# Largest weight over the 128 partitions: by two passes through TensorE, or by a small tensor in memory

## The chip, the cores and the metric

The kernel runs on one core of a Trainium2 chip. The metric is the device time of one execution in microseconds (us). A core has engines that each take their own instructions in order: TensorE (PE, matrix products; PEld is its weight load), VectorE (DVE), ScalarE (ACT), GpSimd (POOL) and SyncE (SP, which here only issues transfers). They wait for each other by semaphores. Transfers between the core's memory and the chip's memory (DRAM) run on 16 DMA engines beside them.

## The reference

A linear recurrence over time (RWKV) gives tokens `x`, and a mixture of 8 experts is applied to every token, weighted by a gate that eight rounds of row and column normalisation (Sinkhorn) balance:

```python
x = attn_out.transpose(0, 2, 1, 3).reshape(3072, 384)      # _attn_ref: recurrence over 768 steps
logits = x @ w_gate                                        # 3072 x 8
P = np.exp(logits - logits.max())
for _ in range(8):
    P /= P.sum(1, keepdims=True) + 1e-09
    P /= P.sum(0, keepdims=True) + 1e-09
    P *= N / E
out = np.zeros((N, D))
for e in range(E):                                         # 8 experts
    h = np.maximum(x @ w1[e], 0.0)                         # 384 x 1024
    out += P[:, e:e + 1] * (h @ w2[e])                     # 1024 x 384
```

## The kernel before

**Numbers.** Products run in 16-bit floats, and each operand is split into a high and a low half (three products for one). So that the halves fit, weights are first scaled by a power of two that follows from the largest absolute weight. The largest value has to be known on all 128 partitions, and this step is the one that changes.

**Stages.** The recurrence comes first and computes expert 0 beside it. Then come 14 stages, one for each half of experts 1 to 7. A stage multiplies tokens and weights in a scheme with 15 products in place of 18 (`g1_slots`: 15 slots of three matmuls each, with VectorE and ScalarE adding up the results from PSUM banks named bA, bY, bZ, bC, bB into `tb`, `hbx`, `hb`), for two groups of tokens `g` and two column halves `j`. That makes 60 slots a stage. Between the slots stand the matmuls of the second product of the group before (`po`), five or four after each slot. Their results are scaled (`stg`) and added to `accd` in DRAM by transfers that POOL issues. The stretch between the end of the recurrence and stage 0 is called the passage below. It works off the rest of expert 0 (`ph`, `po`), runs the Sinkhorn rounds (`rs`, `pc`, `cs`, `pm`) and prepares the first weights and the second group of tokens.

**Order.** Every engine's instructions stand in the order in which the program is written. In a stage, `stage_tasks` hangs the steps for the next stage's weights on slots (`at(19, ...)`). In the passage, a table of `ticks` does the same: a tick runs its steps and then one unit of expert 0, which is nine `ph` or twelve `po` matmuls.

**The next stage's weights** (`stage_weights`), by slot: `load` at 0 (two transfers into `rawb`), `pool` sums into `ucb` on POOL, `amax` at 9, 10, 17, 18 (VectorE, largest of a partition's weights, into `wms`), `reduce_max` at 19 (`wmas`, 128 x 2), `across` at 21, `scale` at 23 (`isw`, `sw`), and from slot 30 on `high` (ScalarE) and `low` (VectorE), which write the two halves into `ws`. `across` and `scale` use `over_partitions`: TensorE transposes `wmas` into two rows of 128 (`pmax_s`), VectorE takes the largest of each row (`mt_s`) and puts the two on a diagonal (`md_s`), and a product with ones brings them to all partitions, from where `scale` reads them. The PSUM bank for this comes from the pool that `small_` names.

**Tokens in the passage** (`plan_tokens`): VectorE puts the halves of tokens together (`rebuild`, `ucb<-hbx`, three times), POOL makes 17 sums from them (`pool`, into `tb`), and ScalarE and VectorE split these in four parts into `xv`. This is done twice in the passage, for token groups 2 and 3, in the same buffers `ucb` and `tb`; the weights of stage 0 use `ucb` in between.

Of the kernel before, what the change touches and what calls it, by code (L numbers as in the profile page):

```python
# [8 lines left out]
F32 = mybir.dt.float32  # L9
# [3 lines left out]
ALU = mybir.AluOpType  # L13
AX = mybir.AxisListType
# [18 lines left out]
def rwkv_sinkhorn_moe(  # L33
# [13 lines left out]
    V, S_, G, T, Q = (  # L47
        InOrder(tc, e) for e in (nc.vector, nc.scalar, nc.gpsimd, nc.tensor, nc.sync)
    )
# [3 lines left out]
    E, _, F = w1.shape  # L53
    P = 128
# [6 lines left out]
    TB = 512  # L61
# [10 lines left out]
    sm = ctx.enter_context(tc.tile_pool(name="sm", bufs=2))  # L72
    stgp = ctx.enter_context(tc.tile_pool(name="stgp", bufs=3))
    dram = ctx.enter_context(tc.tile_pool(name="dram", bufs=1, space=bass.MemoryType.DRAM))
    ps1 = ctx.enter_context(tc.tile_pool(name="ps1", bufs=2, space=PSUM))
    ps2 = ctx.enter_context(tc.tile_pool(name="ps2", bufs=2, space=PSUM))
# [37 lines left out]
        return v_[:, :, t % TH, :]  # L114

    accd = dram.tile([NT, DM], F32, name="accd")
    e0d = [dram.tile([NT, DM], F32, name=f"e0d{j}") for j in range(2)]
    logits = const.tile([P, NTT, E], F32, name="logits")
    inv_s = const.tile([P, NTT], F32, name="inv_s")
# [6 lines left out]
    def pow2_scale(m, inv, s, down):  # L126
        V.tensor_scalar(inv, m, 1e-30, down, op0=ALU.max, op1=ALU.mult)
        V.tensor_single_scalar(
            inv.bitcast(I32), inv.bitcast(I32), EXP_MASK, op=ALU.bitwise_and
        )  # L130
        V.reciprocal(s, inv)


    def over_partitions(m, n, pool, tag, name):

        pt = pool.tile([P, TB], F32, tag=tag, name=f"pmax_{name}")
        T.transpose(pt[:n, :P], m, ident)
        mt = sm.tile([P, 1], F32, tag="mt", name=f"mt_{name}")
        V.tensor_reduce(mt[:n], pt[:n, :P], axis=AX.X, op=ALU.max)
        md = sm.tile([P, 2], F32, tag="md", name=f"md_{name}")  # L140
        V.tensor_scalar_mul(md[:n, :n], ident[:n, :n], mt[:n])
        yield pt[:, 2 * P : 2 * P + n]
        T.matmul(pt[:, 2 * P : 2 * P + n], ones[:n, :], md[:n, :n], start=True, stop=True)
        yield pt[:, 2 * P : 2 * P + n]
# [474 lines left out]
    def add(o, x_, y_):  # L619
        return lambda: G.tensor_tensor(o, x_, y_, op=ALU.add)  # L620

    def sub(o, x_, y_):
        return lambda: G.tensor_tensor(o, x_, y_, op=ALU.subtract)
# [133 lines left out]
    ps4 = ctx.enter_context(tc.tile_pool(name="ps4", bufs=4, space=PSUM))  # L757
# [3 lines left out]
    ucb = big.tile([P, 11 * TS], F32, name="ucb")  # L761
    tb_ = big.tile([P, 13 * TS], F32, name="tb")
# [5 lines left out]
    def stage_weights(s):  # L768
        e, half = 1 + s // 2, s % 2
        home = ws0 if s % 2 == 0 else ws1  # L770
        w1s = part(home, F16, 0, (NPR, 2, TS))
        w2s = part(home, F16, NPR * 2 * TS, (2, FHC, DM))
        isw = sm.tile([P, 2], F32, tag="isw", name=f"isw_{s}", bufs=3)
        sw = sm.tile([P, 2], F32, tag="sw", name=f"sw_{s}")
        m = sm.tile([P, 4], F32, tag="wm", name=f"wms_{s}")
        ma = sm.tile([P, 2], F32, tag="wma", name=f"wmas_{s}")
        uc = part(ucb, F32, 0, (11, TS))

        def load():
            fs = slice(half * FH, (half + 1) * FH)  # L780
            Q.dma_start(raw1, w1[e][:, fs].rearrange("(c p) f -> p c f", p=P))
            Q.dma_start(raw2, w2[e][fs, :].rearrange("(c p) d -> p c d", p=P))

        def amax(i):
            n = KC * FH // 2
            V.tensor_reduce(
                m[:, i : i + 1], rawb[:, i * n : (i + 1) * n],
                axis=AX.X, op=ALU.max, apply_absolute_value=True,
            )

        res = []

        def reduce_max():
            V.tensor_reduce(ma, m.rearrange("p (j i) -> p j i", i=2), axis=AX.X, op=ALU.max)

        def across():
            res.append(over_partitions(ma, 2, *small(), f"s{s}"))
            next(res[0])

        def scale():  # L800
            pow2_scale(next(res[0]), isw, sw, 0.25)

        a = [raw1[:, i % KC, (i // KC) * TS : (i // KC + 1) * TS] for i in range(6)]
        u_ = {r_: uc[:, UI[r_]] for r_ in US[:11]}
        pool = [
            add(u_[0], a[0], a[2]), sub(u_[7], a[3], a[0]), add(u_[1], u_[7], a[4]),
            sub(u_[2], u_[1], a[1]), sub(u_[10], a[2], a[1]), add(u_[3], u_[2], u_[0]),
            sub(u_[8], a[5], u_[10]), add(u_[9], a[3], a[5]), sub(u_[12], a[4], u_[8]),
            sub(u_[13], a[2], a[5]), add(u_[14], a[0], a[5]),
        ]  # L810
        pieces = [
            (w1s[:, i : i + n], uc[:, i : i + n], 0) for i, n in ((0, 3), (3, 3), (6, 3), (9, 2))
        ] + [
            (w1s[:, 11:13], raw1[:, 0:2, :TS], 0), (w1s[:, 13:15], raw1[:, 1:3, TS:], 0)
        ] + [
            (w2s[:, :, i : i + 2].rearrange("p l c d -> p c l d"), raw2[:, i : i + 2], 1) for i in (0, 2)
        ]

        def high(i):
            o, x_, j = pieces[i]  # L820
            S_.activation(o[:, :, 0], x_, AF.Copy, scale=sw[:, j : j + 1])

        def low(i):
            o, x_, j = pieces[i]
            V.scalar_tensor_tensor(
                o[:, :, 1], x_, sw[:, j : j + 1], o[:, :, 0], op0=ALU.mult, op1=ALU.subtract
            )

        return dict(w1s=w1s, w2s=w2s, isw=isw, load=load, amax=amax, reduce_max=reduce_max, across=across,
                    scale=scale, pool=pool, high=high, low=low, n=len(pieces))  # L830


# [38 lines left out]
    def at(t, *fs):  # L871
        ticks.setdefault(t, []).extend(fs)

    small_ = [(ps2, "po")]

    def small():
        return small_[0]

    WS = {0: stage_weights(0)}
    sk = sinkhorn()  # L880
    at(0, WS[0]["load"])
# [7 lines left out]
    def plan_tokens(sg, t_build, t_pool, pool_rate, t_parts, homes):  # L889
        rebuild, singles, pool, high, low = combine_tokens(sg, *homes)  # L890
        for th, t in enumerate(t_build):
            at(t, lambda th=th: rebuild(th))
        at(t_build[-1], singles)
        for i, f in enumerate(pool):
            at(t_pool + i // pool_rate, f)
        for (i, n), t in zip(((0, 3), (3, 3), (6, 3), (9, 4)), t_parts):
            at(t, lambda i=i, n=n: high(i, n))
            at(t + 1, lambda i=i, n=n: low(i, n))

    plan_tokens(2, (0, 1, 2), 3, 3, (5, 7, 8, 10), (ucb, 0, tb_, 0))  # L900
    W0 = WS[0]
    for i, t in enumerate((4, 5, 9, 10)):
        at(t, lambda i=i: W0["amax"](i))
    at(11, W0["reduce_max"])
    at(12, W0["across"])
    for i, f in enumerate(W0["pool"]):
        at(9 + i // 3, f)
    at(14, W0["scale"])
    for n, i in enumerate((0, 1, 2, 3, 4, 5, 6, 7)):
        at(15 + n, lambda i=i: W0["high"](i))  # L910
        at(16 + n, lambda i=i: W0["low"](i))
    plan_tokens(3, (20, 20, 21), 21, 3, (24, 26, 27, 29), (ucb, 0, tb_, 0))

    tick = 0
    while units or any(t >= tick for t in ticks):
# [172 lines left out]
    def stage_tasks(s):  # L1088
        ts = {}

        def at(t, *fs):
            ts.setdefault(t, []).extend(fs)

        def gate():
            pes[s] = gate_of(1 + s // 2, WS[s]["isw"], s)

        at(2, gate)
        if s == 0:
            at(3, gate0)
        if s + 1 < NS:  # L1100
            w_ = WS[s + 1] = stage_weights(s + 1)
            at(0, w_["load"])
            for i, t in enumerate((9, 10, 17, 18)):
                at(t, lambda i=i: w_["amax"](i))
            for i, f in enumerate(w_["pool"]):
                at(8 + i, f)
            at(19, w_["reduce_max"])
            at(21, w_["across"])
            at(23, w_["scale"])
            for i, (th_, tl) in zip(  # L1110
                (4, 6, 0, 7, 1, 5, 2, 3),
                ((0, 2), (1, 3), (8, 9), (8, 10), (15, 17), (16, 18), (23, 24), (23, 25)),
            ):
                at(NSLOT + th_, lambda i=i: w_["high"](i))
                at(NSLOT + tl, lambda i=i: w_["low"](i))
        else:
            for _ in range(2 * FHC):
                at(20, load_final)
        for n in range(4):
            n4 = (s - 2) * 4 + n  # L1120
            if 0 < n4 <= NTT:
                at(15 * n + 2, flush(n4 - 1)[1])
                at(15 * n + 3, flush(n4 - 1)[2])
            if 0 <= n4 < NTT:
                at(15 * n + 8, flush(n4)[0])
        return ts
# [4 lines left out]

    rest = e0_rest()
    late = None
    small_[0] = (ps4, "pq")
    for s in range(NS):
        tasks = stage_tasks(s)
        for g in range(NG):
            for j in range(2):
                for n, nxt in enumerate(g1_slots(s, g, j)):
# [3 lines left out]
                    i = j * NPR + n  # L1143
# [37 lines left out]
```

## Time and profile before

| what | value |
|---|---|
| median of 3 runs | 1607.06 us (1606.31 to 1610.93) |
| the profiled execution | 1606.63 us, of which the span from the first to the last instruction is 1604.9 us |
| TensorE busy | 1575.5 us, 98% of the span |
| VectorE, ScalarE, GpSimd busy | 1019.4, 668.0 and 587.7 us |
| mean granted TensorE clock | 0.991 |

Rows of the profile read like this. In a timeline: start, duration, engine, line, operation, what it writes and reads with the shape, how many alike in a row, and in square brackets the idle time before it with what ended it. In a list of groups: busy time in all, mean ns of one, idle time before them. All work on the compute engines and all transfers of the kernel bear line 29, a helper that records the order, so the names of the tiles tell operations apart. In the list of transfers the last number is the median time from issue to landing, in us.

### The profile page before, as it was taken

How to read it: one execution, taken by the hardware profiler on the slowest of the kernel's cores; microseconds unless marked ns; L12 is line 12 of the kernel's file. 1: busy time of each engine (PE TensorE's matmuls, PEld its weight loads, DVE VectorE, ACT ScalarE, POOL GpSimd, SP SyncE). 2: the span in 40 equal slices, each digit the busy share in tenths (PEclk: the TensorE clock that was granted, in tenths of full speed). 3: DMA queues.
4: the chain of work that ended last, by engine and by line, in shares of the span. 5: the costliest groups of instructions: out<-in, count | busy, mean ns of one | idle time of the engine just before them, and what ended most of it. 6: DMA issues, size and time to landing. Idle time of an engine off the chain costs nothing.

```text
span 1604.9 us, 24284 instructions
## 1 busy us (share of the span) xinstructions
PE 1575.5 (98%) x9423; PEld 912.8 (57%) x9423; DVE 1019.4 (64%) x1706; ACT 668.0 (42%) x1190; POOL 587.7 (37%) x688
## 2 busy tenths in 40 slices
PE   7899999989999999999999999999999999999999
PEld 5777787655455555555555555555555555555555
DVE  6676756674766666666666666666666666656554
ACT  2233333343544445454535454544444453535320
POOL 6566675452020342424242424243242424242200
PEclk8899999999999999999999999999999999999999
DMA  7233330212022556565665656564545454545434
GB/s 181 48 70 76 85 86 26 86 42 89 30 94 55 105 83 115 84 122 84 123 89 85 115 83 120 85 114 58 94 55 94 56 97 54 96 55 89 60 89 132
DMA packets 163899, 136.60 MB, mean 85 GB/s; under 512 B 88257, under 2 KB 158018, under 8 KB 163778
## 3 DMA queue, kind: packets, MB, share of 16 engines
q0 software_dynamic: 44928, 61.36, 30.9%
q1 hardware_dynamic: 118640, 73.63, 15.8%
q8 instruction: 75, 1.23, 0.3%
q14 instruction: 46, 0.38, 0.1%
q10 hardware_dynamic: 210, 0.00, 0.0%
HBM read 53.69 MB, written 80.22 MB: 83 GB/s over the span
## 4 chain that ended last, share of the span: by engine, by line
PE 94%; DVE 3%; ACT 1%; issue 1%; ACTq 0%; DVEq 0%
PE po L29 46%; PE bZ L29 11%; PE bY L29 11%; PE ph L29 5%; PE bB L29 4%; PE bA L29 4%; PE py L29 4%; PE bC L29 2%; PE pA L29 1%; PE pu L29 1%; PE prT L29 1%; PE pz L29 1%; PE pkT L29 1%; DVE ws L29 0%; PE px L29 0%
## 5 line engine op out<-in xcount | busy, mean ns | idle before, releaser
L29 PE MATMUL po<-ws,hbx 128*128 128x384 f16 x3360 | 736.9, 326 | 0.0
L29 POOL DMA_DIRECT2D accd<-stg x288 | 250.4, 870 | 700.7 <-ACT stg L29 682.8
L29 PEld LDWEIGHTS <-hbx 128*128 128x128 f16 x3576 | 337.1, 98 | 287.4
L29 PEld LDWEIGHTS <-ws 128*128 128x128 f16 x3096 | 303.4, 98 | 249.6 <-issue 8.3
L29 ACT ACTIVATE hbx<-tb 128x512 f16<-128x512 f32 x224 | 141.1, 630 | 444.3 <-DVE tb L29 444.3
L29 PE MATMUL po<-ws,hb 128*128 128x384 f16 x1248 | 323.0, 327 | 2.3 <-DVE ws L29 2.3
L29 DVE TENSOR_TENSOR tb<-bY,tb 128x512 f32<-128x512 f32 x168 | 116.2, 692 | 193.9 <-PE bY L29 192.8
L29 ACT ACTIVATE stg<-po,pe 128x384 f32<-128x384 f32 x312 | 179.5, 575 | 127.9 <-PE po L29 101.0
L29 PE MATMUL bZ<-xv,ws 128*128 128x512 f16 x840 | 227.0, 379 | 0.8 <-DVE tb L29 0.7
L29 PE MATMUL bY<-xv,ws 128*128 128x512 f16 x840 | 227.0, 379 | 0.1
L29 DVE TENSOR_TENSOR tb<-bZ,tb 128x512 f32<-128x512 f32 x168 | 115.5, 687 | 133.1 <-PE bZ L29 133.1
L29 PEld LDWEIGHTS <-hb 128*128 128x128 f16 x1248 | 122.4, 98 | 96.1 <-issue 4.9
L29 POOL TENSOR_TENSOR ucb<-rawb 128x256 f32<-128x256 f32 x84 | 75.1, 945 | 94.0 <-DMA rawb<-in_moe_w_dram 94.0
L29 DVE TENSOR_TENSOR tb<-bB,tb 128x512 f32<-128x512 f32 x112 | 77.5, 692 | 49.7 <-PE bB L29 47.8
L29 PE MATMUL ph<-hbx,ws 128*128 128x384 f16 x576 | 106.1, 333 | 1.2 <-DVE hb L29 1.2
L29 DVE SCALAR_TENSOR_TENSOR hbx<-tb,hbx 128x512 f16<-128x512 f32 x112 | 78.6, 702 | 24.2 <-ACT hbx L29 19.5
L29 DVE SCALAR_TENSOR_TENSOR hb<-tb,hbx 128x512 f16<-128x512 f32 x112 | 77.2, 690 | 24.6 <-ACT hbx L29 19.5
L29 PE MATMUL bA<-xv,ws 128*128 128x512 f16 x336 | 90.8, 379 | 1.0 <-ACT tb L29 1.0
L29 PE MATMUL bB<-xv,ws 128*128 128x512 f16 x336 | 90.8, 379 | 0.0
L29 DVE SCALAR_TENSOR_TENSOR hb<-ph,hb 128x384 f16<-128x384 f32 x64 | 35.5, 555 | 60.8 <-ACT hb L29 60.6
L29 ACT COPY tb<-bZ 128x512 f32<-128x512 f32 x56 | 32.8, 586 | 68.2 <-PE bZ L29 68.2
L29 ACT ACTIVATE hb<-ph 128x384 f16<-128x384 f32 x64 | 31.5, 492 | 60.3 <-PE ph L29 59.0
(163 smaller groups left out, 1647.6 us busy)
## 6 DMA issues: line engine op xcount, KB each, us to landing
accd<-stg POOLq DMA_DIRECT2D x288, 192.0 KB, 3.7
rawb<-in_moe_w_dram SPq DMA_DIRECT2D x28, 768.0 KB, 7.4
e0d<-stg SPq DMA_DIRECT2D x48, 192.0 KB, 2.0
hb<-e0d SPq DMA_DIRECT2D x48, 192.0 KB, 3.4
rn<-in_r_dram SPq DMA_DIRECT2D x24, 192.0 KB, 3.1
kn<-in_k_dram SPq DMA_DIRECT2D x24, 192.0 KB, 3.3
vn<-in_v_dram SPq DMA_DIRECT2D x24, 192.0 KB, 2.7
accd<-stg SPq DMA_DIRECT2D x24, 192.0 KB, 1.8
```

Of the source, the lines that this page charges most:

```text
L29: return lambda *a, **k: self.tc.keep_in_program_order(f(*a, **k))
```

## The change

For the 14 stages, `over_partitions` is no longer used (the gate, the maximum of the logits and expert 0's own weights keep it). `reduce_max` now also starts a transfer on SP that writes `wmas` to a DRAM tensor `wmx` of its own for each stage: 256 elements of 4 bytes. `across` is a second transfer on SP, which reads those 256 numbers back into each of the 128 partitions (1 KB each), in a part of `tb` that the stages leave free. It waits for the first to land. `scale` has VectorE take the two maxima from the 256 numbers (`wmj`) and goes on as before. In a stage the steps stand at slots 19, 20 and 25 instead of 19, 21 and 23. In the passage they stand at ticks 10, 11 and 15 instead of 11, 12 and 14; `high` and `low` of stage 0's weights and the second `plan_tokens` stand one tick later.

```diff
+    wmx = dram.tile([2 * E, 2, P], F32, name="wmx")
...
-        res = []
+        mb = tb_[:, 5 * TB : 5 * TB + 2 * P]
 
         def reduce_max():
             V.tensor_reduce(ma, m.rearrange("p (j i) -> p j i", i=2), axis=AX.X, op=ALU.max)
+            Q.dma_start(wmx[s].rearrange("j p -> p j"), ma)
 
         def across():
-            res.append(over_partitions(ma, 2, *small(), f"s{s}"))
-            next(res[0])
+            Q.dma_start(
+                mb, wmx[s].rearrange("(o j) p -> o (j p)", o=1).broadcast_to([P, 2 * P])
+            )
 
         def scale():
-            pow2_scale(next(res[0]), isw, sw, 0.25)
+            mj = sm.tile([P, 2], F32, tag="wmj", name=f"wmj_{s}")
+            V.tensor_reduce(mj, mb.rearrange("p (j q) -> p j q", q=P), axis=AX.X, op=ALU.max)
+            pow2_scale(mj, isw, sw, 0.25)
...
-    at(11, W0["reduce_max"])
-    at(12, W0["across"])
+    at(10, W0["reduce_max"])
+    at(11, W0["across"])
...
-    at(14, W0["scale"])
+    at(15, W0["scale"])
...
-    plan_tokens(3, (20, 20, 21), 21, 3, (24, 26, 27, 29), (ucb, 0, tb_, 0))
+    plan_tokens(3, (21, 21, 22), 22, 3, (25, 27, 28, 30), (ucb, 0, tb_, 0))
...
-            at(21, w_["across"])
-            at(23, w_["scale"])
+            at(20, w_["across"])
+            at(25, w_["scale"])
```

VectorE in the passage, before, from the last `amax` on (`hb<-ph` splits a result of expert 0, `xv<-tb` a part of the tokens, `rs` begins a Sinkhorn round):

```order
L29 TENSOR_REDUCE wms_6990<-rawb 128x1
L29 SCALAR_TENSOR_TENSOR hb_73<-ph_5_7207,hb_73 128x384
L29 TENSOR_TENSOR xv_6983<-tb,xv_6983 128x4x256
L29 TENSOR_REDUCE wmas_6991<-wms_6990 128x2
L29 TENSOR_REDUCE rs_7240<-pm 128x24
```

The same place now:

```order
L29 TENSOR_REDUCE wms_6991<-rawb 128x1
L29 TENSOR_REDUCE wmas_6992<-wms_6991 128x2
L29 SCALAR_TENSOR_TENSOR hb_73<-ph_5_7210,hb_73 128x384
L29 TENSOR_TENSOR xv_6984<-tb,xv_6984 128x4x256
L29 TENSOR_REDUCE rs_7243<-pm 128x24
```

`wmas` has moved ahead of two instructions, and TensorE, which had its transposition of `wmas` between two units of expert 0, has nothing there now.

VectorE later in the passage, before (`ws<-rawb` are `low` steps of stage 0's weights, `ucb<-hbx` the three `rebuild` steps of the second `plan_tokens`, `cs` to `pm` half a Sinkhorn round):

```order
L29 TENSOR_TENSOR ucb<-hbx 128x2x3x128 x2
L29 SCALAR_TENSOR_TENSOR ws_74<-rawb,sw_6989,ws_74 128x2x256
L29 TENSOR_TENSOR ucb<-hbx 128x2x3x128
L29 SCALAR_TENSOR_TENSOR hb_73<-ph_3_7428,hb_73 128x384
L29 TENSOR_REDUCE cs_7442<-pc_7440 128x8
L29 TENSOR_SCALAR cs_7442<-cs_7442 128x8
L29 RECIPROCAL cs_7442<-cs_7442 128x8
L29 TENSOR_TENSOR pm<-pm,cs_7442 128x192
L29 SCALAR_TENSOR_TENSOR ws_74<-rawb,sw_6989,ws_74 128x768
L29 SCALAR_TENSOR_TENSOR hb_73<-ph_4_7452,hb_73 128x384
L29 SCALAR_TENSOR_TENSOR ws_74<-rawb,sw_6989,ws_74 128x768
L29 TENSOR_REDUCE rs_7484<-pm 128x24
```

The same place now:

```order
L29 TENSOR_TENSOR ucb<-hbx 128x2x3x128 x2
L29 SCALAR_TENSOR_TENSOR hb_73<-ph_3_7416,hb_73 128x384
L29 TENSOR_REDUCE cs_7430<-pc_7428 128x8
L29 TENSOR_SCALAR cs_7430<-cs_7430 128x8
L29 RECIPROCAL cs_7430<-cs_7430 128x8
L29 TENSOR_TENSOR pm<-pm,cs_7430 128x192
L29 SCALAR_TENSOR_TENSOR ws_74<-rawb,sw_6990,ws_74 128x2x256
L29 TENSOR_TENSOR ucb<-hbx 128x2x3x128
L29 SCALAR_TENSOR_TENSOR hb_73<-ph_4_7445,hb_73 128x384
L29 SCALAR_TENSOR_TENSOR ws_74<-rawb,sw_6990,ws_74 128x768
L29 TENSOR_REDUCE rs_7478<-pm 128x24
```

The third `rebuild` stands behind an `hb` and a `cs` group that it stood ahead of, and the last `low` has gone behind the `rs` that ends this piece.

VectorE at slots 19 to 25 of a stage, before:

```order
L29 TENSOR_REDUCE wmas_9125<-wms_9124 128x2
L29 TENSOR_TENSOR tb<-bZ_0_1_9336,tb 128x512
L29 SCALAR_TENSOR_TENSOR hbx<-tb,hbx 128x512
L29 TENSOR_TENSOR tb<-bC_0_1_9390,tb 128x512
L29 TENSOR_REDUCE mt_s_9398<-pmax_s_9396 2x1
L29 TENSOR_SCALAR md_s_9400<-ident,mt_s_9398 2x2
L29 TENSOR_TENSOR tb<-bY_0_1_9325,tb 128x512
L29 SCALAR_TENSOR_TENSOR hbx<-tb,hbx 128x512
L29 TENSOR_TENSOR tb<-bZ_0_1_9336,tb 128x512
L29 TENSOR_SCALAR isw_9122<-pmax_s_9396 128x2
L29 TENSOR_SCALAR isw_9122<-isw_9122 128x2
L29 RECIPROCAL sw_9123<-isw_9122 128x2
```

The same place now:

```order
L29 TENSOR_REDUCE wmas_9117<-wms_9116 128x2
L29 TENSOR_TENSOR tb<-bZ_0_1_9328,tb 128x512
L29 SCALAR_TENSOR_TENSOR hbx<-tb,hbx 128x512
L29 TENSOR_TENSOR tb<-bC_0_1_9384,tb 128x512
L29 TENSOR_TENSOR tb<-bY_0_1_9317,tb 128x512
L29 SCALAR_TENSOR_TENSOR hbx<-tb,hbx 128x512
L29 TENSOR_TENSOR tb<-bZ_0_1_9328,tb 128x512
L29 TENSOR_REDUCE wmj_9435<-tb 128x2
L29 TENSOR_SCALAR isw_9114<-wmj_9435 128x2
L29 TENSOR_SCALAR isw_9114<-isw_9114 128x2
L29 RECIPROCAL sw_9115<-isw_9114 128x2
```

`mt_s` and `md_s` are gone and `wmj` is new. Although `scale` is written two slots later, it stands behind the same `tb<-bZ` as before, since VectorE has no other work in those two slots.

SP in the same stage now (`hb<-e0d` fetches a piece of expert 0's result; before, the two middle rows were not there):

```order
L29 DMA hb_73<-e0d_79 128x384
L29 DMA hb_73<-e0d_80 128x384
L29 DMA wmx<-wmas_9117 128x2x1
L29 DMA tb<-wmx 128x256
L29 DMA hb_73<-e0d_79 128x384
```

The fetches behind the new pair now stand behind the wait of `tb<-wmx` for the landing of `wmx`. GpSimd's instructions stand as before.

More of the change, by code (lines that the diff above doesn't have):

```diff
@@ L872, in at @@
         ticks.setdefault(t, []).extend(fs)
-    small_ = [(ps2, "po")]
-    def small():
-        return small_[0]
     WS = {0: stage_weights(0)}
@@ L903, in rwkv_sinkhorn_moe @@
         at(t, lambda i=i: W0["amax"](i))
-    at(11, W0["reduce_max"])
-    at(12, W0["across"])
+    at(10, W0["reduce_max"])
+    at(11, W0["across"])
     for i, f in enumerate(W0["pool"]):
         at(9 + i // 3, f)
-    at(14, W0["scale"])
+    at(15, W0["scale"])
     for n, i in enumerate((0, 1, 2, 3, 4, 5, 6, 7)):
-        at(15 + n, lambda i=i: W0["high"](i))
-        at(16 + n, lambda i=i: W0["low"](i))
-    plan_tokens(3, (20, 20, 21), 21, 3, (24, 26, 27, 29), (ucb, 0, tb_, 0))
+        at(16 + n, lambda i=i: W0["high"](i))
+        at(17 + n, lambda i=i: W0["low"](i))
+    plan_tokens(3, (21, 21, 22), 22, 3, (25, 27, 28, 30), (ucb, 0, tb_, 0))
     tick = 0
@@ L1133, in rwkv_sinkhorn_moe @@
     late = None
-    small_[0] = (ps4, "pq")
     for s in range(NS):
```

## The prediction, made before the change was run

> **What bounds the kernel now.** I read the page's summary and its chain of waits first, then the waits of TensorE, then busy times by stretch, then the timelines around the step that changes.
>
> ```profile
> span 1604.9 us, 24284 instructions
> PE 1575.5 (98%) x9423; PEld 912.8 (57%) x9423; DVE 1019.4 (64%) x1706; ACT 668.0 (42%) x1190; POOL 587.7 (37%) x688
> PE 94%; DVE 3%; ACT 1%; issue 1%; ACTq 0%; DVEq 0%
> PE pmax_s L29 <- DVE wmas L29: 4.2, 2, 3.2
> 487.00:1450.00 963.00, 963.00 (x5265) 515.01 (x5264) 613.59 (x956) 445.29 (x783) 336.81 (x408) 1.00 0.56 88
> ```
>
> TensorE holds 94% of the chain that ended last. From 487 to 1450 us (last row: the first number after the length is TensorE's) it is never idle, at the full clock (the 1.00). There time is TensorE's own instructions and nothing else. The fourth row is one of its waits elsewhere (total, times, longest): 4.2 us, in two places, for `wmas`, the input of the transposition that the change removes. So three places count: the 12 saturated stages, the passage, and stage 0.
>
> **A, the saturated stages.** 14 sets of weights pass through the step: one in the passage (323 us), one in stage 0 (408 us), the other 12 at 488.6 to 1436.5 us, one each stage. TensorE in the first of these:
>
> ```profile
> 485.21 0.81 PE L29 MATMUL bY<-xv,ws 128*128 128x512 f16 x3
> 485.86 0.33 PE L29 MATMUL po<-ws,hb 128*128 128x384 f16 x1
> 487.97 0.81 PE L29 MATMUL bC<-xv,ws 128*128 128x512 f16 x3
> 488.72 0.33 PE L29 MATMUL po<-ws,hb 128*128 128x384 f16 x1
> 491.00 0.81 PE L29 MATMUL bZ<-xv,ws 128*128 128x512 f16 x3
> 492.05 0.34 PE L29 MATMUL po<-ws,hbx 128*128 128x384 f16 x1
> L29 PE MATMUL pmax_s<-ident,wmas x14: 269/272/273, 323.1 to 1436.5; 128*2 128x128 f32 x14
> ```
>
> Durations overlap, so I go by starts. Three 512-column matmuls to the next `po` take 0.65 us without the step, 0.75 with the transposition between, 1.05 with the product with ones. The step costs 0.10 + 0.40 = 0.5 us; from unrounded starts 0.51. Twelve stages: **-6.1 us**, since nothing else is waited for there, provided the replacement causes no wait.
>
> The replacement: SP writes 256 elements of 4 bytes, waits, reads 1 KB into each partition; then VectorE does `wmj` and three small operations before its next work.
>
> ```profile
> wt<-in_w_dram SPq DMA_DIRECT2D x1, 0.8 KB, 2.1
> e0d<-stg SPq DMA_DIRECT2D x48, 192.0 KB, 2.0
> accd<-stg POOLq DMA_DIRECT2D x288, 192.0 KB, 3.7
> DMA to landing us min/median/max: 2.4/3.4/7.3
> ub<-in_u_dram SPq DMA_DIRECT2D x1, 192.0 KB, 4.8
> 918.33 0.14 DVE L29 TENSOR_REDUCE wmas<-wms 128x2 f32<-128x4 f32 x1
> 927.41 0.69 DVE L29 TENSOR_TENSOR tb<-bZ,tb 128x512 f32<-128x512 f32 x1 [3.54 <-PE bZ L29]
> 929.41 0.81 PE L29 MATMUL bZ<-xv,ws 128*128 128x512 f16 x3
> L29 DVE TENSOR_REDUCE rs<-pm 128x24 f32<-128x192 f32 x8 | 2.7, 341 | 0.0
> L29 DVE TENSOR_REDUCE dg<-rk 128x8 f32<-128x384 f32 x24 | 13.0, 542 | 0.0
> L29 DVE TENSOR_REDUCE mt_s<-pmax_s 2x1 f32<-2x128 f32 x14 | 3.8, 269 | 0.0
> L29 DVE TENSOR_SCALAR md_s<-ident,mt_s 2x2 f32<-2x2 f32 x14 | 3.2, 228 | 0.5
> ```
>
> No row shows this write. It lies between 2.0 us (`e0d<-stg`, rows of 1.5 KB into DRAM) and 3.7 (`accd<-stg`, where memory is read and written); I take 2.1, the only transfer of single 4-byte elements (`wt`, 192 of them). The read lies between 2.4 and 4.8: the row with three numbers is `hb<-e0d`, reads of 1.5 KB into each partition in these stages, and `ub` is the one read that spreads one piece over all partitions, early among other loads. I take the median of the former, 3.4. With an estimated 0.2 for two hand-overs the round trip is **5.7 us**, ends 4.6 and 8.7. `wmj` takes 0.41 us, between 341 ns for 192 elements and 542 for 384; `isw`, `isw`, `sw` follow in about 0.5. VectorE saves 0.27 + 0.23 on `mt_s` and `md_s`, so its own work is even.
>
> The time available: `wmas` ends at 918.47 and the next work of VectorE, which would otherwise sit idle 3.54 us, starts at 927.41, earlier by 0.51 now. Less 0.9 for the four operations, 7.5 us remain, and 5.7 fits. Beyond that the first to be late is `tb<-bZ`, which ends at 928.1 and is needed by TensorE at 929.41: another 1.3 us, so TensorE waits only from a round trip of 8.8. Queued behind the wait on SP are fetches (`hb<-e0d`) whose consumer stands at slot 32, nine slots later; in stage 1 stores of `stg`, which has three buffers. The pair's issues cost SP some 0.8 us a stage, at a time when it idles. POOL's queue is unmoved. The freed PSUM bank brings nothing: no wait of TensorE in these stages names a bank.
>
> The page "DMA: Bandwidth & Descriptors" of the Trainium skill (section Specifications) says that transfers below 512 bytes are read, modified and written, which speaks against 4-byte writes. Taking the 3.7 us of the accumulating row for that, the round trip would be 7.3, still inside 7.5 here, and 1.6 us worse in part C below; nothing in this trace shows such a write.
>
> **B, the passage.** Here TensorE waits 3.24 us for `wmas`:
>
> ```profile
> 317.72 2.11 PE L29 MATMUL po<-ws,hb 128*128 128x384 f16 x12
> 323.07 0.27 PE L29 MATMUL pmax_s<-ident,wmas 128*2 128x128 f32 x1 [3.24 <-DVE wmas L29]
> 323.85 0.49 DVE L29 TENSOR_TENSOR pm<-pm,rs 128x192 f32<-128x192 f32 x1
> 329.88 3.10 PE L29 MATMUL ph<-hbx,ws 128*128 128x384 f16 x18
> 340.00:350.00 10.00, 10.00 (x63) 6.12 (x62) 9.42 (x19) 5.92 (x10) 3.46 (x4) 1.00 0.28 85
> 352.71 0.56 PE L29 MATMUL pc<-pm,ones 128*128 128x192 f32 x2 [2.02 <-DVE pm L29]
> 350.60:353.90 3.30, 1.28 (x8) 0.86 (x8) 3.20 (x8) 0.48 (x1) 3.14 (x4) 1.00 0.16 60
> 354.00:357.30 3.30, 3.30 (x12) 1.54 (x11) 2.12 (x6) 1.22 (x2) 3.22 (x5) 0.50 0.00 0
> 401.80:405.10 3.30, 2.28 (x11) 0.89 (x10) 3.20 (x6) 1.64 (x4) 0.00 (x0) 1.00 0.00 0
> 346.54 3.60 POOL L29 TENSOR_TENSOR tb<-ucb 128x256 f32<-128x256 f32 x4 [18.89 <-DVE ucb L29]
> 362.64 1.04 ACT L29 CAST xv<-tb 128x1024 f16<-128x1024 f32 x1 [2.09 <-POOL tb L29]
> 365.69 1.22 DVE L29 TENSOR_TENSOR xv<-tb,xv 128x1024 f16<-128x1024 f32 x1
> 368.72 0.56 PE L29 MATMUL pc<-pm,ones 128*128 128x192 f32 x2 [0.16 <-DVE pm L29]
> ```
>
> Without the transposition the next `ph` starts at 319.7, when the twelve `po` have been issued (a little over 0.16 us each; the 18 of the fourth row take 3.10 with the last one's end), and nine `ph` and twelve `po` keep TensorE until 323.1. Then stands `pc`, which needs `pm`. VectorE has the same instructions ahead of that `pm` as before, in another order, so it ends at 324.35 as in the third row. TensorE waits 1.3 us and, behind a `pc` of 0.3, the `ph` x18 of 329.88 starts at 324.65: 5.2 us gained.
>
> What is late next? VectorE, 9.42 us busy in 10. I laid its rows up to 353 us in the new order, one behind the other. The `pm` that ended the wait at 352.71 now comes at 347.3, and TensorE arrives at 345.3: a wait of 2.0 as before, gain 5.4. But the third `rebuild` now stands behind `hb` and a `cs` group and ends at 344.0, and POOL's sums start there, only 2.5 us earlier than at 346.54. They and the cast took 17.1 us (346.54 to 363.68): the cast ends at 361.1, then VectorE's `xv`, `hb` and `rs` group take 3.0 (365.69 to 368.72) and the `pc` that stood at 368.72 starts at 364.2. There the gain falls to **4.5 us**; TensorE waits 3.0 us for it if it came at full clock, 1.3 if it had slowed after 347.3.
>
> The clock (the last but two column of the rows with a stretch): after 3.3 us in which TensorE was busy for 1.28, the granted clock was 0.50 for as long, 1.7 us lost; after 2.28 busy it stayed at 1.00. If the 2.0 us wait loses the clock again, the later wait absorbs it and leaves about 2.0 busy, nearer to the row that kept it. If not, the later wait of 3.0 loses it. I charge half a loss, 0.8: **B = -3.7 us**, ends -5.4 (POOL faster, clock kept) and -1.1 (clock lost twice).
>
> The Trainium skill, "TensorE: Matmul & The Clock Gate", section What's actually happening, has the half clock after an idle window of about 3.4 us; the trace shows it after a wait of 2.02, so I go by the trace. By the page none of my waits would count, and B would be -4.5.
>
> **C, stage 0.** Here `po` has run out, slots are short, and VectorE is the slower engine:
>
> ```profile
> 407.75 0.15 DVE L29 TENSOR_REDUCE wmas<-wms 128x2 f32<-128x4 f32 x1
> 413.02 0.69 DVE L29 TENSOR_TENSOR tb<-bZ,tb 128x512 f32<-128x512 f32 x1 [0.50 <-PE bZ L29]
> 413.76 0.81 PE L29 MATMUL bZ<-xv,ws 128*128 128x512 f16 x3
> ```
>
> From 407.9 a round trip of 5.7 and 0.9 for the four operations put the next `tb<-bZ` at 414.5 in place of 413.02, and TensorE's `bZ` at 413.76 starts as it ends. The saved transposition waits (1.0 and 0.8) don't help, as VectorE sets the pace: **+1.5 us**, ends +0.4 and +4.5, and 1.7 more if the clock falls.
>
> **Sum.** -6.1 - 3.7 + 1.5 = -8.3 us against the profiled execution's own 1606.63 us (span 1604.9 and 1.7 around it), which lies 0.4 below the median of the runs: **1598.3 us**, 0.5% faster.
>
> **Rivals.**
>
> - *The round trip is too long, and the kernel gets slower.* One mechanism: `wmj` waits, `tb<-bZ` is late, TensorE stops in every stage. It costs from 8.8 us on and outweighs A from 9.3. For it: with the 7.3 of the slowest `hb<-e0d` for the read and 3.7 for the write, 11.2 us, each stage loses 2.4, twelve lose 29, stage 0 some 7, B stays: 1606.6 + 29 + 7 - 6.1 - 3.7 = 1633. Against it: the median is 3.4. 6%.
> - *All of the gain stays.* POOL finishes early enough and stage 0 hides the trip: -6.1 - 5.4 + 0.4 = -11.1, 1595.5. Against it: POOL's 17 us are measured. 20%.
> - *The passage and stage 0 give back what they gain.* B -1.1, C +4.5: -2.7, 1603.9, within 0.3%. For it: both places hang on VectorE, and late work there costs the clock too. 17%.
> - *My sum.* 57%.
>
> **How the numbers follow.** A measurement of this kernel tells about 0.3%, 4.8 us, from no change. The range takes in the second and third rival nearly whole and leaves the slow one out: 1594.5 to 1604.5. My sum and the second rival are faster by more than 0.3%, the third is the same, the first slower: 0.77 faster, 0.17 same, 0.06 slower.
>
> **What would show it.** Right: the stages' period on TensorE shorter by 0.51 us; `wmj` starting without idle time ended by a transfer, except in stage 0; `ph` following `po` at once near 320 us; a wait of `pc` for `pm` near 364. Wrong: TensorE waiting for `tb` in the stages, or `wmx` landing later than 3.7 us, or the passage ending at the same time as before.

## The result, and the profile after

| | before | after |
|---|---|---|
| median of 4 runs | 1608.99 us (1606.31 to 1611.34) | 1710.1 us (1708.31 to 1713.12) |
| profiled execution, span | 1604.9 us | 1706.6 us |
| TensorE busy | 1575.5 us (98%) | 1594.0 us (93%) |
| mean granted clock | 0.991 | 0.970 |

The ratio is 1.0644 (1.0621 to 1.0667): the change costs 101 us where 8 were to be gained. One execution is left out of the ratios: the kernel with the later scale below took 2348 us once, at a granted clock of 0.651. The page of the changed kernel, summary and chain of waits, the groups of instructions, and the list of transfers (last number: median us from issue to landing):

```profile
span 1706.6 us, 24227 instructions
PE 1594.0 (93%) x9381; PEld 912.8 (53%) x9381; DVE 1022.8 (60%) x1692; ACT 667.6 (39%) x1190; POOL 587.0 (34%) x688
PE 79%; DMA 12%; DVE 6%; POOL 1%; issue 1%; ACT 1%; DVEq 0%; SPq 0%; POOLq 0%; ACTq 0%
...
L29 DVE TENSOR_REDUCE wmj<-tb 128x2 f32<-128x256 f32 x14 | 5.9, 420 | 134.1 <-DMA tb<-wmx 134.1
...
tb<-wmx SPq DMA_DIRECT2D x14, 128.0 KB, 5.1
...
wmx<-wmas SPq DMA_DIRECT2D x14, 1.0 KB, 9.4
```

Transfers were nowhere in the chain before and are 12% of it now; TensorE falls from 94% to 79%. VectorE sits idle 134 us ahead of its 14 `wmj`. The write takes 9.4 us and the read 5.1. The waits of the same kernel (total, times, longest), and one of the saturated stages in its timeline:

```profile
PE bZ L29 <- DVE tb L29: 81.3, 16, 9.8
```

```profile
875.71 0.14 DVE L29 TENSOR_REDUCE wmas<-wms 128x2 f32<-128x4 f32 x1
875.88 0.37 SPq L29 DMA_DIRECT2D wmx<-wmas  x1
879.98 0.69 DVE L29 TENSOR_TENSOR tb<-bZ,tb 128x512 f32<-128x512 f32 x1 [0.17 <-PE bZ L29]
884.13 0.32 SPq L29 DMA_DIRECT2D tb<-wmx  x1
889.60 0.42 DVE L29 TENSOR_REDUCE wmj<-tb 128x2 f32<-128x256 f32 x1 [8.92 <-DMA tb<-wmx]
890.54 0.69 DVE L29 TENSOR_TENSOR tb<-bZ,tb 128x512 f32<-128x512 f32 x1
891.28 1.44 PE L29 MATMUL bZ<-xv,ws 128*128 128x512 f16 x3 [4.85 <-DVE tb L29]
```

The write is issued at 875.88, the read 8.25 us later, and 5.5 us after that `wmj` starts. It stands ahead of `tb<-bZ` in VectorE's queue, so that is late, and TensorE's `bZ` waits 4.85 us. It then runs slowly: three matmuls take 1.44 us where the same three took 0.81. Busy time by stretch shows why. The last three columns are the granted clock, the share of the transfers' engines and GB/s; the first row is a stretch of full speed, the second follows the wait, and the third is stage 0, from the write's issue to its landing:

```profile
487.00:500.00 13.00, 13.00 (x73) 6.96 (x72) 7.07 (x10) 5.40 (x11) 0.51 (x1) 1.00 0.17 62
891.20:894.60 3.40, 3.32 (x11) 1.41 (x11) 2.01 (x4) 2.07 (x4) 0.73 (x1) 0.57 0.00 0
410.70:419.00 8.30, 3.74 (x16) 1.45 (x15) 3.73 (x6) 1.76 (x3) 0.00 (x0) 1.00 0.02 0
```

After the wait the clock was 0.57 for 3.4 us. In the third row the share of the transfers' engines is 0.02, so almost nothing else was moving, and still the write took 8.3 us. There it was not waiting behind other traffic.

Where the 101.7 us between the two spans lie, from the starts of the first `pc`, the first `bA` and the `wmas` in both traces:

| stretch | before | after | difference |
|---|---|---|---|
| start to the first `pc` | 308.78 | 306.00 | -2.8 |
| passage, to the first `bA` | 75.45 | 81.00 | +5.6 |
| stage 0, to the `wmas` of stage 1 | 103.23 | 114.50 | +11.3 |
| 11 stages, to the last `wmas` | 947.91 | 1027.87 | +80.0 |
| the rest | 169.56 | 177.24 | +7.7 |

The first row is no effect of the change: over the profiles below, in which nothing in that stretch differs but one early transfer in one of them, the first `pc` starts between 303.65 and 312.44 us.

### The profile page after: what moved, and what is told of

The parts are those of the page before. It is cut to its first block, busy times and chain, and to the rows that moved or that the text cites. A ratio compares the mean times of both kernels' runs of the same rounds, so it can differ in the third digit from the quotient of the medians.

```text
span 1706.6 us, 24227 instructions
## 1 busy us (share of the span) xinstructions
PE 1594.0 (93%) x9381; PEld 912.8 (53%) x9381; DVE 1022.8 (60%) x1692; ACT 667.6 (39%) x1190; POOL 587.0 (34%) x688
## 4 chain that ended last, share of the span: by engine, by line
PE 79%; DMA 12%; DVE 6%; POOL 1%; issue 1%; ACT 1%; DVEq 0%; SPq 0%; POOLq 0%; ACTq 0%
PE po L29 38%; PE bZ L29 10%; PE bY L29 9%; DMA wmx<-wmas 8%; PE bA L29 4%; DMA tb<-wmx 4%; PE ph L29 4%; PE bB L29 4%; PE py L29 4%; DVE tb L29 2%; PE bC L29 2%; PE pA L29 1%; PE pu L29 1%; POOL tb L29 1%; PE prT L29 1%
## 5 line engine op out<-in xcount | busy, mean ns | idle before, releaser
L29 PE MATMUL po<-ws,hbx 128*128 128x384 f16 x3360 | 746.2, 329 | 0.0
L29 PEld LDWEIGHTS <-hbx 128*128 128x128 f16 x3576 | 341.1, 99 | 299.4 <-issue 13.6
L29 PE MATMUL po<-ws,hb 128*128 128x384 f16 x1248 | 327.4, 331 | 3.8 <-DVE ws L29 2.3
L29 PE MATMUL bZ<-xv,ws 128*128 128x512 f16 x840 | 235.1, 390 | 81.3 <-DVE tb L29 81.3
L29 PE MATMUL bB<-xv,ws 128*128 128x512 f16 x336 | 95.2, 394 | 0.0
L29 DVE TENSOR_REDUCE wmj<-tb 128x2 f32<-128x256 f32 x14 | 5.9, 420 | 134.1 <-DMA tb<-wmx 134.1
```

The source lines that it names most:

```text
L29: return lambda *a, **k: self.tc.keep_in_program_order(f(*a, **k))
```

## The experiments

**First probe: transfers that nobody waits for.** Beside the kernel before, ten kinds of small transfers in turn:

```diff
+        if s > 0:
+            at(26, lambda: probe(2 * s - 2))
+            at(44, lambda: probe(2 * s - 1))
```

> The kernel before with its step on TensorE, and beside it 26 transfers that nobody waits for, ten kinds in turn in stages 1 to 13, to see from issue to landing what a small transfer takes by itself. In the changed kernel the write of 256 elements of 4 bytes landed after 9.4 us (median), though its packets took 9 ns each and were all done 1.1 us after the issue; the read landed after 5.1. Theories: (T1) the pieces go to one kilobyte of DRAM and follow each other there: 256 x 4 bytes 9 us, 128 pieces 5 to 6, and 2 to 3 when each piece has 512 bytes of its own. (T2) each small piece costs by itself, wherever it goes: 9 us for 256 pieces spread or not, 5 to 6 for 128. (T3) any write of pieces of a few bytes takes 9 us, whatever their count, and one piece of 1 KB 2.1. (T4) it is the company in the changed kernel: all land after 2 to 4 us here, the 256 x 4 bytes too. For the read: if 128 partitions that fetch the same kilobyte get in each other's way, 1 KB each from 128 rows lands after about 3.4 and the same kilobyte after 5; if it is the amount, both land alike and the read of 8 bytes each near 2.4. Time of the kernel: within 0.3% of before, since nothing waits for them.

The time was 1603.6 us in one run (1606.2 before). SP had nothing to wait for and issued nine of the 26 right behind 1.5 MB of weights and twelve behind two fetches of 192 KB, so most landings, those of the reads among them, tell of these as well. The list of transfers has the following (three issued of each; the trace has three, two and one landing):

```profile
pv<-ones SPq DMA_DIRECT2D x3, 1.0 KB, 8.8
pj<-ones SPq DMA_DIRECT2D x3, 1.0 KB, 8.9
pvs<-ones SPq DMA_DIRECT2D x3, 1.0 KB, 3.1
```

`pv` is the change's write, in a kernel without the rest of the change: it lands late here too (8.0 and 8.8 where no weights were ahead), so T4, the company, falls. `pvs`, the same 256 pieces with 512 bytes for each, landed after 3.1, the one time that shows. So neither the count of pieces nor their 4 bytes alone is slow. `pj`, 128 pieces of 8 bytes, landed after 4.4 where no weights were ahead and 13.5 behind them: inconclusive, and left to the next run.

**Pieces of 8 bytes.** The same 1 KB, laid out so that the two numbers of a partition are neighbours:

```diff
-    wmx = dram.tile([2 * E, 2, P], F32, name="wmx")
+    wmx = dram.tile([2 * E, P, 2], F32, name="wmx")
...
-            Q.dma_start(wmx[s].rearrange("j p -> p j"), ma)
+            Q.dma_start(wmx[s], ma)
```

> The changed kernel with the two maxima of a partition side by side in memory, so that its write is 128 elements of 8 bytes in place of 256 of 4. By T1 and T2 (time goes with the count) the write lands after 5 to 6 us, the round trip falls from about 14 to about 10.5, and each of 14 stages loses about 3.5 to 4 us less: about 1710 - 50 = 1655 us. By T3 (a fixed price) the write stays at 9 us and the time at 1710.

1608.45 us, ratio 1.0006 (0.9986 to 1.0027): the loss of 101 us is gone with this one edit, twice as much as T1 and T2 had for half the pieces. Its list of transfers, and two of its stages in the timeline:

```profile
tb<-wmx SPq DMA_DIRECT2D x14, 128.0 KB, 5.0
...
wmx<-wmas SPq DMA_DIRECT2D x14, 1.0 KB, 3.4
```

```profile
665.01 0.15 DVE L29 TENSOR_REDUCE wmas<-wms 128x2 f32<-128x4 f32 x1
675.67 0.42 DVE L29 TENSOR_REDUCE wmj<-tb 128x2 f32<-128x256 f32 x1 [5.70 <-DMA tb<-wmx]
677.36 0.81 PE L29 MATMUL bZ<-xv,ws 128*128 128x512 f16 x3 [1.62 <-DVE tb L29]
...
1186.34 0.15 DVE L29 TENSOR_REDUCE wmas<-wms 128x2 f32<-128x4 f32 x1
1194.49 0.42 DVE L29 TENSOR_REDUCE wmj<-tb 128x2 f32<-128x256 f32 x1 [3.19 <-DMA tb<-wmx]
```

The write takes 3.4 us instead of 9.4, the read 5.0 as before. In the second stage shown the trip from `wmas` to `wmj` is 8.0 us and TensorE does not wait; in the first, with more transfers beside it (a share of 0.88 of their engines, against 0.57), 10.5 and a wait of 1.6.

**The scale later.** The change's own slow write, for the saturated stages only (`MEM(s)` chooses the sets that go through memory), but `scale` at slot 30, where the change has 25. The first two `high` and `low` steps stand two slots later. Excerpts, against the kernel before:

```diff
+    def MEM(s):
+        return s >= 2
...
-            at(23, w_["scale"])
+            at(30 if MEM(s + 1) else 23, w_["scale"])
...
-                ((0, 2), (1, 3), (8, 9),
+                ((2, 4), (3, 5), (8, 9),
```

> Only the 12 sets of weights of the saturated stages go through memory; the passage and stage 0 keep TensorE's transpositions. The write and the read start at slots 19 and 20 as in the change, but the scale is taken at slot 30 in place of 25, some 7 us later, and the first two high and low parts two slots later. If VectorE's wait for the round trip is all that the stages lose, the window grows from 7.5 to 14.7 us (16.0 until TensorE waits), which covers most round trips of 13.5 to 15.3, and the 0.51 us a stage of the step on TensorE is what is left: 1609.0 - 6.1 = 1603, at most some us more. If the transfers cost something by their being there, or the step on TensorE was hidden by other things, the time is 1609 or above.

1600.61 us, ratio 0.9964 (0.9946 to 0.9983): 5.6 us less than the 1606.23 beside it, as the wait theory had it. Its transfers are nearly as slow as the change's, and nobody waits:

```profile
tb<-wmx SPq DMA_DIRECT2D x12, 128.0 KB, 4.9
...
wmx<-wmas SPq DMA_DIRECT2D x12, 1.0 KB, 8.8
```

```profile
996.72 0.14 DVE L29 TENSOR_REDUCE wmas<-wms 128x2 f32<-128x4 f32 x1
1011.59 0.41 DVE L29 TENSOR_REDUCE wmj<-tb 128x2 f32<-128x256 f32 x1
```

`wmj` has no wait in brackets. A stage takes 85.65 us in all 11 periods, 0.52 below the 86.17 of before. So the slow write costs these stages nothing by its being there; their whole loss is the wait for it, and what the wait does to the clock.

**The passage alone.** The ticks are the change's, all later sets go by TensorE.

```diff
+    def MEM(s):
+        return s == 0
```

> Only the passage is changed, as in the change: the first set of weights goes through memory with the moved ticks, all later sets use TensorE as before. My prediction had -3.7 us for this part (ends -5.4 and -1.1), 1605.3. The trace of the changed kernel has stage 0 begin 2.8 us later than before while the tick with the last recurrence product stood 2.7 us earlier, and VectorE waiting 5.9 us for the read: if that wait is the price, +3 to +5.5 us, 1612 to 1614.5.

1607.14 us, ratio 1.0003 (0.9987 to 1.0019): neither my -3.7 nor the +3 to +5.5 read from the changed kernel's trace. In its profile the passage took 78.40 us from the first `pc` to the first `bA`, 2.95 above before, inside the interval (up to +3.1). The changed kernel has the same order and 81.00. The two traces show where its 2.6 us more lie: `wmas` starts 0.9 later behind the first `pc` (13.42 and 12.50), the trip is 0.8 longer (13.55 and 12.73), and the other 0.9 come behind `wmj`, where the clock was half for 6.8 us there and for 3.4 here.

**Second probe: how the pieces lie.** Sixteen writes of eight kinds, each with a read that waits for it, in stages 1 to 12.

```diff
+        if 1 <= s <= 8:
+            at(20, lambda: probe(s - 1, 0))
+        elif 9 <= s <= 12:
+            at(20, lambda: probe(s - 9, 1))
+            at(40, lambda: probe(s - 5, 1))
```

> The kernel before with its step on TensorE, and in stages 1 to 12 sixteen writes to DRAM, eight kinds twice, each followed by a read of its first number that waits for it, so that each landing shows. Known so far: 256 pieces of 4 bytes side by side land after 8 to 11 us, 128 pieces of 8 bytes side by side after 2.8 to 5.4, 256 pieces of 4 bytes with 512 bytes for each after 3.1 (one landing). Theories: (W1) pieces of 4 bytes that share 8 bytes with another piece are slow: 128, 64 or 16 pieces of 4 bytes side by side land late (8 us, fewer pieces perhaps sooner), the same pieces at every eighth byte after about 3. (W2) pieces of 4 bytes that lie in the same longer stretch are slow: at every eighth byte still 8, at every 64th byte about 3. (W3) it is the number of pieces alone: 64 pieces 4 to 5 and 128 pieces 5 to 6 us, side by side or not. By each the pieces of 8 bytes land after about 3.

1603.2 us in one run (1606.2 before). Eleven of the sixteen writes failed as in the first probe: SP ran ahead and issued them behind weights or right behind two fetches of 192 KB. Clear of both stand the first write, 128 pieces of 4 bytes side by side, which landed after 8.1 us, and the second ones of stages 9 to 12, each behind a read that had waited: 256 pieces side by side after 10.8, 256 at every eighth byte 4.2, 64 side by side 7.4, 16 side by side 2.0. By W3, the count alone, the two with 256 would be alike.

**Two faster versions.** Pieces of 8 bytes, `scale` at slot 30 and the changed passage; the set of stage 0 goes by TensorE in the first (its `MEM` is shown), through memory in the second.

```diff
+    def MEM(s):
+        return s != 1
```

> Pieces of 8 bytes, the scale at slot 30 in place of 25 in the saturated stages, the changed passage, and TensorE's transpositions for the one set in stage 0. From the profiles so far: the 12 saturated stages gain 0.52 each (-6.3), the passage with the short write 2.2 (from the first gate product to stage 0 it took 73.2 us with pieces of 8 bytes, 75.5 before), stage 0 nothing: about -8.5 us, 1597.7 beside 1606.2, ratio 0.9947. If the passage's gain was chance, -6.3: ratio 0.9961. It would be slower than that if the later scale makes ScalarE late for the stages, which the run with the later scale did not show.

> As the kernel with TensorE's transpositions kept in stage 0, but the set in stage 0 goes through memory too, with its scale at slot 30. With the scale at slot 25 stage 0 lost 4.6 us (from its first product to the next stage's maxima 107.8 us with pieces of 8 bytes, 103.2 before). If that loss was VectorE's wait for the round trip, slot 30 hides it and the time is that of the sister kernel within 2 us, about 1598; if the transfer or the order itself costs, it is some 4 us above it.

They took 1596.01 us, ratio 0.9934 (0.9914 to 0.9954), and 1596.44 us, 0.9932 (0.991 to 0.9954): some 0.7% faster than before, the best of this study, and alike. In both profiles the saturated periods are 85.65 us (two neighbours in the second 86.0 and 85.3). From the first `pc` to the first `bA` the passage takes 73.21 and 72.34 us (75.45 before); stage 0 of the second takes 102.85 us (103.23 before). With pieces of 8 bytes and slot 25 stage 0 took 107.79, so there too the loss was VectorE's wait.

**Pieces of 4 bytes at every eighth byte.** The change as it is, with gaps between the pieces (and one early transfer that fills the gaps):

```diff
+    wmx = dram.tile([2 * E, P, 2, 2], F32, name="wmx")
...
+            Q.dma_start(wmx[s][:, :, :1], ma.unsqueeze(2))
```

> The changed kernel, all 14 sets and the scale at slot 25, with its 256 pieces of 4 bytes at every eighth byte of 2 KB, so that the count stays and no two pieces share 8 bytes; the read brings 2 KB to each partition in place of 1, and the maxima skip the gaps. (W1) the write lands after about 3 us; the read, 5.0 us for 1 KB, takes 5 to 7.5 for 2 KB: round trip 8.5 to 11, a stage between its gain of 0.52 and a loss of 4: 1605 to 1655 us. (W2) or (W3): the write stays at 8 to 11 us and the time at 1710 or up to 30 us above it for the longer read.

1625.83 us, ratio 1.0117 (1.0088 to 1.0145), inside W1's range, though its write took 4.9 us and not about 3. With 256 pieces of 4 bytes as in the change, the other layout brings the write from 9.4 to 4.9:

```profile
tb<-wmx SPq DMA_DIRECT2D x14, 256.0 KB, 4.7
wmx<-wmas SPq DMA_DIRECT2D x14, 1.0 KB, 4.9
```

The layout differs from the change's in two things: the gaps, and that the two numbers of a partition are now neighbours. The next probe separates them, with one number of each partition.

**Third probe: chains that start from the stage's maxima.** This cures the fault of the other two: the first write of a chain waits for `wmas`, so it is issued clear of weights and fetches. It is not alone, though I had expected that: while the writes were under way, the share of the transfers' engines was 0.47 to 0.91, with POOL's stores of `stg` among them.

```diff
+            if 9 <= s <= 12:
+                at(20, w_["chain"])
```

> The kernel before with its step on TensorE; in stages 9 to 12, where no other store is under way, twelve chains on SP that start from the stage's own maxima: a write to DRAM, a read of its first number that waits for it, one of four reads into the core (1 KB to 128 partitions from one row, the same amount from 128 rows, 8 bytes to 128 partitions, 1 KB to one partition), and a last write that waits for that read. The runs so far: the 256 pieces of 4 bytes at every eighth byte land after 3.4 to 5.7 us, side by side after 8 to 11; pieces of 8 bytes side by side after 2.8 to 5.4. (W1) slow are pieces of 4 bytes that share 8 bytes with another: 256, 128 and 64 side by side about 8, 32 between, 16 some 2 to 3.5; 128 at every 8th, 16th and 64th byte, 128 and 64 of 8 bytes, and 16 at every eighth byte 2.5 to 3.5 each, 256 at every eighth 3.5 to 5. (W2) slow are pieces that share a longer stretch: at every 8th and 16th byte near 8 as well, at every 64th about 3. For the reads: if one row for 128 partitions is the price, it lands after 5 and 128 rows after 3 to 3.5; if it is the amount, both land after 5. Time of the kernel: within 0.5% of before.

One run, 1610.98 us beside 1607.36 before. The time of a write is read from its issue to that of the read that waits for it, in the queue's timeline (names: count, bytes of a piece, and how they lie, "c" for side by side):

```profile
1181.37 0.37 SPq L29 DMA_DIRECT2D wa256x4c<-wmas  x1
1190.08 0.31 SPq L29 DMA_DIRECT2D tb<-wa256x4c  x1
1194.10 0.36 SPq L29 DMA_DIRECT2D tb<-e0d  x1
1197.33 0.24 SPq L29 DMA_DIRECT2D chw<-tb  x1
1197.61 0.34 SPq L29 DMA_DIRECT2D wb128x8c<-wmas  x1
1201.31 0.23 SPq L29 DMA_DIRECT2D tb<-wb128x8c  x1
1204.52 0.33 SPq L29 DMA_DIRECT2D tb<-e0d  x1
1206.77 0.24 SPq L29 DMA_DIRECT2D chw<-tb  x1
...
1366.59 0.33 SPq L29 DMA_DIRECT2D wh128x4at<-wmas  x1
1369.81 0.23 SPq L29 DMA_DIRECT2D tb<-wh128x4at  x1
...
1449.71 0.33 SPq L29 DMA_DIRECT2D wk128x4at<-wmas  x1
1451.26 0.23 SPq L29 DMA_DIRECT2D tb<-wk128x4at  x1
```

The first two pairs give 8.7 us for the change's write and 3.7 for pieces of 8 bytes. All twelve, one landing each:

| pieces | side by side | every 8th byte | every 16th | every 64th |
|---|---|---|---|---|
| 256 of 4 bytes | 8.7 | 5.3 | | |
| 128 of 4 bytes | 8.5 | 5.3 | 3.2 | 1.6 |
| 64 of 4 bytes | 7.1 | | | |
| 32 of 4 bytes | 6.2 | | | |
| 16 of 4 bytes | 1.7 | 2.4 | | |
| 128 of 8 bytes | 3.7 | | | |
| 64 of 8 bytes | 5.4 | | | |

The 128 pieces, one a partition, fall from 8.5 to 1.6 us as they move apart, so the gaps matter by themselves and W3 falls. They fall gradually, where W1 and W2 had a step, so neither rule is right in its words: the distance from one piece to the next moves the time most. It is not all: side by side the count moves it too, from 1.7 us for 16 pieces (2.0 in the second probe) to 8.7 for 256, and 64 pieces of 8 bytes took more than 128. What happens in the memory stays open. For the reads (`tb<-e0d` to `chw<-tb`): 1 KB from one row to 128 partitions 3.2 to 3.4 us, the same amount from 128 rows 2.1 to 2.3. So one row for all partitions costs about 1.1 us, but that does not reach the 5.1 of the change's read, which fetches what has just been written. That this is the reason was not tested; the chains' reads of one number just written took between 1.1 and 4.0 us.

## Why the prediction was wrong, step by step

**The step that failed is a term of A: the price of the write.** I had 2.1 us, from the only transfer of 4-byte elements in the trace. That was a read of 192 elements, and this is a write; my upper bound of 3.7 came from a store whose pieces have 1.5 KB. It measured 9.4. The read was mis-sized too, 5.1 where I took 3.4 (ends 2.4 and 4.8). From `wmas` to `wmj` the saturated stages show 13.7 to 15.4 us; I had 5.7 with ends of 4.6 and 8.7, and so counted on no wait there. The range rested on these ends, and a bound from the nearest row is no bound when the row differs from the new thing in kind: nothing in the trace wrote small pieces side by side.

**The window around it was right.** I put the trip from which TensorE waits at 8.8 us and the gain of a stage without a wait at 0.51. Three kernels with `scale` at slot 25 give 33 periods with trips of many lengths, of which these are examples (the 8.75 of the last column is read from them):

| kernel | trip, `wmas` to `wmj` | period | 85.65 + (trip - 8.75) |
|---|---|---|---|
| 8 bytes | 7.8 to 8.3 (5 stages) | 85.65 | |
| 8 bytes | 9.01 | 85.92 | 85.91 |
| 8 bytes | 10.51 | 87.43 | 87.41 |
| every eighth byte | 10.87 | 87.97 | 87.77 |
| every eighth byte | 11.07 | 89.85 | 87.97 |
| after | 13.74 | 92.05 | 90.64 |
| after | 15.28 | 95.13 | 92.18 |

(Trips from the end of `wmas` to the start of `wmj`; periods from one `wmas` to the next.) With trips up to 8.3 us the stage takes 0.52 us less than the 86.17 of before. Above 8.75, the trip costs its excess one for one, within 0.4 us in every period with a trip up to 10.9. `wmj` was 0.42 us (0.41 foreseen); with the gaps it was 0.61, which is the 0.2 that the row of 10.87 lies above the line.

**A term that was missing: the clock, once per stage.** The last three rows lie 1.4 to 3.0 us above the straight line. The kernel with gaps shows where it sets in:

```profile
589.80 0.81 PE L29 MATMUL bZ<-xv,ws 128*128 128x512 f16 x3 [2.36 <-DVE tb L29]
...
1031.91 0.81 PE L29 MATMUL bZ<-xv,ws 128*128 128x512 f16 x3 [2.50 <-DVE tb L29]
```

```profile
589.80:593.20 3.40, 3.40 (x12) 1.48 (x12) 1.96 (x3) 2.07 (x4) 0.82 (x1) 0.62 0.00 0
...
1031.90:1035.30 3.40, 3.39 (x18) 1.76 (x18) 2.70 (x5) 2.17 (x5) 0.81 (x1) 1.00 0.00 0
```

A wait of 2.36 us was followed by a clock of 0.62, one of 2.50 by the full clock. The records of the clock tell why. In each of the eleven profiles it changes only at times that lie whole multiples of 3.41 us apart. From 80 us on, a step of that grid at full clock was always followed by half the clock when TensorE was busy in it for 1.40 us or less, and never when it was busy for 1.50 or more. The wait of 2.36 lay within one step and left it 1.05 busy (587.19 to 590.60); that of 2.50 was split between two, with 1.91 and 2.41 busy. I charged the clock in B and C and left it out of the rival for the stages. In the changed kernel it was half for 3.4 to 10.2 us in each of the 12 stages. With their mean trip of 14.67 us, the excess is 5.9 us, what lies above the line 1.9, less the gain of 0.52: 7.3 a stage, 88 us in all. That is the first rival, which I gave 6%; I had priced it with a trip of 11.2 and no clock, 1633 us.

**B, the passage.** That `ph` follows `po` at once held (at 317.33 in the changed kernel, with no gap). Then VectorE waits 5.85 us for the read ahead of `pm`, and `pc` another 4.19 for that: +5.6 in place of -3.7. With pieces of 8 bytes the passage gained 2.2 us in two profiles and 3.1 in a third, inside my ends of -5.4 and -1.1. My account of it was not right all the same. The first kernel with pieces of 8 bytes and the late scale, and behind it the same place in the run of the passage alone:

```profile
324.06 0.56 PE L29 MATMUL pc<-pm,ones 128*128 128x192 f32 x2 [1.92 <-DVE pm L29]
324.46 4.77 PE L29 MATMUL ph<-hbx,ws 128*128 128x384 f16 x18
...
348.20 0.56 PE L29 MATMUL pc<-pm,ones 128*128 128x192 f32 x2 [1.25 <-DVE pm L29]
...
365.38 0.56 PE L29 MATMUL pc<-pm,ones 128*128 128x192 f32 x2 [0.38 <-DVE pm L29]
```

```profile
322.14 0.56 PE L29 MATMUL pc<-pm,ones 128*128 128x192 f32 x2 [1.93 <-DVE pm L29]
322.54 3.09 PE L29 MATMUL ph<-hbx,ws 128*128 128x384 f16 x18
```

The first wait, 1.3 us foreseen, is 1.92, and the clock falls right there: the 18 `ph` take 4.77 us where they took 3.10. Behind a wait of 1.93 in the other run it held, and in the second kernel with the late scale behind one of 2.29, so this loss hung on how the wait met the grid. The last `pc`, which I had behind POOL's sums with 3.0 or 1.3 us, waits 0.38.

**C, stage 0.** +11.3 us where I had +1.5 with ends of +0.4 and +4.5. It is the same mis-sized write: the trip was 13.6 us, and `bZ` came 15.4 us after `wmas` in place of 6.0, with the clock at half for 10.2 us around it. With pieces of 8 bytes the trip is 7.0 us and stage 0 loses 4.6. `bZ` comes 8.8 us after `wmas` in place of 6.0, which is 2.8, and the other 1.8 are about the clock loss of 1.7 that I kept as an extra.

**The rules that I weighed.** The Trainium skill's page "DMA: Bandwidth & Descriptors" (section Specifications) has transfers below 512 bytes read, modified and written. I let it raise the trip to 7.3, too little. The section does not say how much, and the boundary is not the one that decides here: pieces of 4 and of 8 bytes are both below 512, and side by side they took 9.4 and 3.4 us. The same page of the Trainium skill (section Anatomy of one DMA — SWDGE (gpsimd) path) is on transfers that GpSimd issues, while SP issued these. It puts most of such a transfer's fixed time of about 2 us down to waiting for the memory's receipt, and says that this "can cause a surprisingly long delay especially when the write target is HBM". The trace has the delay at that place: in stage 0 the packets of the changed kernel's write took 9 ns each and were all done 1.1 us after the issue, and the landing came at 8.3. No run shows what the memory does in between.

The Trainium skill's page "TensorE: Matmul & The Clock Gate" (section What's actually happening) has the half clock after an idle window of about 3.4 us that runs freely. The traces agree with the window's length and that it runs freely (the grid of 3.41 us above); they do not agree that it has to be idle, as steps with up to 1.49 us of work were followed by half the clock.

## What to carry to other kernels

A round trip through memory for a few numbers is priced by its write, and that by how the pieces lie there more than by their bytes or count: give a partition's numbers one neighbouring piece, or space the pieces out, before believing a 2 us figure. Find the trip from which the critical engine waits, as from VectorE's idle time here, and if the trip's price has no row of the same kind (direction, size of piece, layout), move its consumer later by several times the estimate; five slots turned the stages' 88 us of loss into 6 of gain here. And a stall on TensorE of some 2 us can cost the clock as well (1.92 us did once, 2.50 once did not), at each place where it returns; those of 4.9 us and more in the changed kernel all did.

## What the hardware showed that I had not expected

- 1 KB written to DRAM as 256 pieces of 4 bytes side by side landed after 8.2 to 11.0 us in the changed kernel (14 landings) and 7.6 to 9.5 with the later scale (11 that show); as 128 pieces of 8 bytes after 2.6 to 5.4 in three kernels (41); as 256 pieces of 4 bytes at every eighth byte after 3.4 to 5.7 (11 that show). 128 pieces of 4 bytes at every 64th byte took 1.6 in a chain, once.
- Reading one row of 1 KB into 128 partitions took 3.2 to 3.4 us, 128 rows of that size 2.1 to 2.3; behind a write of the same row 3.4 to 5.8 in the changed kernel, 5.1 in the median.
- After TensorE's waits of 4.9 to 6.5 us in the changed kernel's saturated stages the granted clock stayed at half long enough to cost 1.3 to 3.0 us more.
- The granted clock changed only on a grid of 3.41 us, and between 1.40 and 1.50 us of work in a step decided whether the next ran at half. So two waits of 1.92 and 1.93 us could end differently: they left 1.49 and 1.58 us of work in their steps.
